# Top 32 of each score row by pair maxima: where the pair minima are made, and which slots search so

## Chip, cores and metric

One core of one Trainium2 chip runs the whole kernel. The metric is device time in microseconds of one execution; lower is better. In the profile the engines are PE (TensorE matmul), PEld (TensorE weight load), DVE (VectorE), ACT (ScalarE), POOL (GpSimd) and SP (the queue that issues most DMAs).

## The reference

Attention in which each query keeps its 32 largest scores, and behind it a two-layer network with a quick GELU. All data are float32.

```python
# q, k, v: (8 batches, 8 heads, 576 positions, 64)
scores = (1 / sqrt(64)) * q @ k.T                      # per batch and head: 576 x 576
kth = np.partition(scores, -32, axis=-1)[..., -32:-31]  # the 32nd largest of each row
scores = np.where(scores >= kth, scores, -1e9)
attn = exp(scores - rowmax);  attn = attn / (rowsum + 1e-9)
x = (attn @ v), heads side by side                     # (4608, 512)
h = x @ w_in                                           # w_in: (512, 2048)
out = (h / (1 + exp(-1.702 * h))) @ w_out              # w_out: (2048, 512)
```

## The kernel before

**Slots.** The attention is cut into 144 slots, 18 for each batch. A slot is 128 query rows of a pair of heads, so it has two score tiles of 128 x 576 (index `i` is 0 or 1). For each slot the kernel makes, in this order:

- `scores(n)` (L297): matmuls into PSUM; `copy_scores(n)` (L309): ScalarE copies them, scaled, into `sc[n]`, two halves `i` of 576.
- The search for the 32 largest scores of each row, on VectorE. MAX8 gives the eight largest of a row, MATCH_REPLACE8 (after a MATCH_VALUE_LOAD) overwrites those eight with a lowest value, so that the next MAX8 finds the next eight.
- `bounds(n)`: two tiny operations on GpSimd that make `cut` (minus the 32nd largest) and `low` (32nd minus largest). `mask(n)` (L426, ScalarE, needs `cut`) and `exps(n)` (L434, ScalarE, needs `low`) make the exponentials `pr` and their row sums `den`.
- `invert(n)` (L442, L444): two tiny VectorE operations turn `den` into `rden`.
- Then normalizing and turning the rows. Up to slot 10 this is `divide` (L451, GpSimd, a diagonal matrix) and matmuls with it; from slot 11 it is `normalize` (L457, GpSimd), `split` (L493, ScalarE), a DMA of `rows` to DRAM and a transposing DMA back into `pt` (L501).
- `values` or `values_at` (L560): matmuls with v.

When four head pairs of a row block are done, the network runs on it in pieces: `hidden` (L621, matmuls with `w_in`), `tanh` (L643, ScalarE, and L646, a copy `h` out of PSUM), `gate` (L655 and L656 on GpSimd, or L658 on VectorE up to slot 10), `project` (L676, matmuls with `w_out`).

**Two kinds of search.** The plain one, `topk`, searches rows of 576: four MAX8 for each half, with three removals between them, the first from `sc` into a tile `left`. It serves slots 0 and 3 to 10. The search by pairs serves slots 1, 2 and 11 to 143 (`by_pairs`). Column k of the first 288 and column k of the last 288 of a row are a pair. `pair_up` makes the pairs' maxima (`greater`) on VectorE (L338), and the minima (`lesser`) on GpSimd in integer arithmetic: a subtract (L342) and, by `pair_rest`, an add (L352). `topk_of_pairs` finds the 32 largest of the maxima (four MAX8 of 288 for each half, three removals) and the 16 largest of the minima (two MAX8, one removal), and joins both lists with two TENSOR_REDUCE: `merge` (L376) and `bound` (L381). `lows` (L402) replaces `bounds` there.

**Order.** The program order on every engine is the order in which the Python code runs (a manual schedule); engines meet only by semaphores. Slots 0 to 10 are issued by `slot(n)`, one after another, with the weights of the network loaded and re-scaled beside them: a raw piece comes by DMA into a buffer of the pool `raws`, ScalarE makes size, sign and low parts (L153, L155, L156), VectorE shifts (L154), GpSimd adds and multiplies (L146, L149; `finish_one`). From slot 11 `two_slots(n)` issues two slots at a time, n odd: `find(n)` and `find(n + 1)` are the searches. Inside `find`, `invert(m - 1)` is put between the searches' operations at a fixed place (`i == 18` or `20` of 23), and `pair_up(m + 1)` too, after the last search of the maxima. In the GpSimd queue of `find(m)` and `measure(m)` stand, in this order, the subtract for m + 1, `normalize(m - 1)`, `lows(m)`, the add for m + 1 and the gate. After slot 143 `last_slot` finishes what is left of the network.

Of the kernel before, what the change touches and what calls it, by code (L numbers as in the profile page):

```python
# [9 lines left out]
ALU = mybir.AluOpType  # L10
# [20 lines left out]
def kernel(  # L31
# [51 lines left out]

    TURNS = 4
    SETTLED = 10
    PAIRED = SETTLED + 1
    EARLY = (1, 2)
    by_pairs = lambda n: n in EARLY or PAIRED <= n < N
    assert D == 64 and 2 * TAIL == P and C == NP * P and C == PIECE and B % 2 == 0
    assert TOPK == 32 and NP == 4 and NF == 4 and NG == 4 and CC == 4  # L90

    const = ctx.enter_context(tc.tile_pool(name="const", bufs=1))
    pool = lambda name, bufs, **kw: ctx.enter_context(tc.tile_pool(name=name, bufs=bufs, **kw))
    raws = pool("raws", 7)
    loads = pool("loads", 2)
    vals = pool("vals", 4)
    qkt = pool("qkt", 6)
    scp = pool("scp", 4)
    prp = pool("prp", 2)
    lefts = pool("lefts", 2)  # L100
    small = pool("small", 4)
    ptp = pool("ptp", 2)
    xs = const.tile([P, 5, CC, P], F32, name="xT")
# [200 lines left out]
    def copy_scores(n):  # L304
        ps = st[n].pop("ps")
        sc = st[n]["sc"] = scp.tile([P, 2, S], F32, name="sc")
        for i in range(2):
            to = sc[:, i, :].rearrange("p (c k) -> p c k", c=2)
            nc.scalar.mul(out=to, in_=ps[i][:, :, 0:HALF], mul=SCALE)  # L309

    def topk(n):

        sc = st[n]["sc"]
        top = st[n]["top"] = small.tile([P, 2, TOPK], F32, name="top")
        left = [lefts.tile([P, S], F32, name="left") for _ in range(2)]
        of = lambda r, i: left[i][:] if r else sc[:, i, :]

        def largest(r, i):
            nc.vector.max(top[:, i, 8 * r : 8 * r + 8], of(r, i))  # L319

        def remove(r, i):
            nc.vector.match_replace(left[i][:], top[:, i, 8 * r : 8 * r + 8], of(r, i), LOWEST)  # L322

        ops = []
        for r in range(TOPK // 8):
            ops += [lambda r=r, i=i: largest(r, i) for i in range(2)]
            if r < TOPK // 8 - 1:
                ops += [lambda r=r, i=i: remove(r, i) for i in range(2)]
        return ops

    greater, lesser = {}, {}

    def pair_up(n):

        sc = st[n]["sc"]
        a, b = sc[:, :, 0:HALF], sc[:, :, HALF:S]
        greater[n] = lefts.tile([P, 2, HALF], F32, name="greater", tag="left")
        nc.vector.tensor_tensor(out=greater[n][:], in0=a, in1=b, op=ALU.max)  # L338
        home, tag = (scp, "sc") if n in EARLY else (raws, "raw")
        lesser[n] = home.tile([P, 2, HALF], F32, name="lesser", tag=tag)  # L340
        whole = lesser[n][:].bitcast(I32)
        nc.gpsimd.tensor_tensor(out=whole, in0=a.bitcast(I32), in1=greater[n][:].bitcast(I32), op=ALU.subtract)  # L342
        unpaired.append(n)

    unpaired = []

    def pair_rest():

        while unpaired:
            n = unpaired.pop()  # L350
            whole, b = lesser[n][:].bitcast(I32), st[n]["sc"][:, :, HALF:S]
            nc.gpsimd.tensor_tensor(out=whole, in0=whole, in1=b.bitcast(I32), op=ALU.add)  # L352

    def topk_of_pairs(n):

        top = st[n]["top"] = small.tile([P, 2, 2 * TOPK], F32, name="top2", tag="top")
        cut = st[n]["cut"] = small.tile([P, 2], F32, name="cut")
        first, few = greater.pop(n), lesser.pop(n)
        left = lefts.tile([P, 2, HALF], F32, name="left2", tag="left")

        def found(r, i, written=False):
            if r < TOPK // 8:
                at = (8 * r + TOPK) % (TOPK + TOPK // 2)
                return top[:, i, at : at + 8]
            end = 2 * TOPK - 8 * (r - TOPK // 8) - TOPK
            return top[:, i, end - 1 : end - 9 : -1] if written else top[:, i, end - 8 : end]

        def largest(src, r, i):
            nc.vector.max(found(r, i, True), src[:, i, :])  # L369

        def remove(to, src, r, i):
            nc.vector.match_replace(to[:, i, :], found(r, i), src[:, i, :], LOWEST)  # L372

        def merge():
            both = top[:, :, 0:TOPK].rearrange("p i (s k) -> p i k s", s=2)
            nc.vector.tensor_reduce(  # L376
                out=top[:, :, TOPK + TOPK // 2 :], in_=both, axis=mybir.AxisListType.X, op=ALU.max
            )

        def bound():  # L380
            nc.vector.tensor_reduce(  # L381
                out=cut[:], in_=top[:, :, TOPK + TOPK // 2 - 1 :], axis=mybir.AxisListType.X, op=ALU.min, negate=True
            )

        ops = []
        for r in range(TOPK // 8):
            ops += [lambda r=r, i=i: largest(left if r else first, r, i) for i in range(2)]
            if r < TOPK // 8 - 1:
                ops += [lambda r=r, i=i: remove(left, left if r else first, r, i) for i in range(2)]
        ops += [lambda: pair_up(n + 1) if PAIRED < n + 1 < N else None]  # L390
        for r in range(TOPK // 8, TOPK * 3 // 16):
            ops += [lambda r=r, i=i: largest(few, r, i) for i in range(2)]
            if r == TOPK // 8:
                ops += [lambda r=r, i=i: remove(few, few, r, i) for i in range(2)]
        return ops + [merge, bound]

    def lows(n):

        top, cut = st[n]["top"], st[n]["cut"]
        low = st[n]["low"] = small.tile([P, 2], F32, name="low")  # L400
        for i in range(2):
            nc.gpsimd.tensor_scalar(  # L402
                low[:, i : i + 1], cut[:, i : i + 1], top[:, i, TOPK : TOPK + 1], -1.0, op0=ALU.add, op1=ALU.mult
            )

    def bounds(n):

        if by_pairs(n):
            return lows(n)
        top = st[n]["top"]  # L410
        cut = st[n]["cut"] = small.tile([P, 2], F32, name="cut")
        low = st[n]["low"] = small.tile([P, 2], F32, name="low")
        nc.gpsimd.tensor_scalar(cut[:], top[:, :, TOPK - 1], -1.0, None, op0=ALU.mult)  # L413
        nc.gpsimd.tensor_tensor(out=low[:], in0=top[:, :, TOPK - 1], in1=top[:, :, 0], op=ALU.subtract)
# [364 lines left out]
    def opening():  # L779

        stay_warm(8, v_ends[0][:].rearrange("p j d -> p (j d)"))
        load("q", 0, 0, nc.sync)
        load("k", 0, 0, nc.scalar)
        for hp in range(2):
            for name in "qk":
                if hp:
                    load(name, 0, hp)
        for x in by_slot[0]:
            load_piece(x)
        prepare_first()  # L790
        scores(0)
        copy_scores(0)
        stay_warm(2)
        for name in "qk":
            prepare(name, 0, 1)
        early.extend(round_piece(x) for x in by_slot[0])
        for piece in early:
            piece["size"]()
        scores(1)
        copy_scores(1)  # L800
        prepare_rest()
        for hp in range(2, NP):
            for name in "qk":
                load(name, 0, hp)
        load_v(0, 0)
        for x in by_slot[1]:
            load_piece(x)
# [11 lines left out]
    def slot(n):  # L819
# [7 lines left out]
        if n == 0:  # L827
            for piece in some:
                piece["low"]()
                piece["sign"]()  # L830
        else:
            if not by_pairs(n):
                bounds(n - 1)
            exponentials(n - 1, bring_all if n % 4 == 1 and n > TURNS + 1 else lambda: None)
            if n == TURNS + 1:
                bring_all()
            copy_scores(n + 1)
            bring_all()
            while signs:
                signs.pop(0)()  # L840
            if 1 < n <= TURNS:
                turn_main(n - 2)
                turn_ends(n - 2)
            for piece in some:
                piece["size"]()
            tanh(False)
        for i, op in enumerate(topk_of_pairs(n) if n in EARLY else topk(n)):
            op()
            if i == 2:
                for _ in range(min(3 if n >= TURNS else 6, len(unfinished))):  # L850
                    finish_one()
            if i == (10 if n in EARLY else 5):
                if n > 0:
                    divide(n - 1)
                while unfinished:
                    finish_one()
            if i == (13 if n == TURNS + 1 else 10):
                gate(False)
        if by_pairs(n + 1):
            bounds(n)  # L860
            pair_up(n + 1)
            pair_rest()
        for piece in some:
            piece["shift"]()
            unfinished.extend(piece["finish"])
# [47 lines left out]
    def two_slots(n):  # L913
# [17 lines left out]
                    fn(*args)  # L931

        def find(m):
            for i, op in enumerate(topk_of_pairs(m) if live(m) else [lambda: None] * 23):
                op()
                if i == (18 if m % 2 else 20) and live(m - 1):
                    invert(m - 1)
                if i > 1 and len(unfinished) > (2 if m == SETTLED + 1 else 0):
                    finish_one()

        def measure(m):
            if live(m):
                lows(m)
            if opens and m == n:
                finish_one()
                finish_one()
                pair_rest()
                return
            pair_rest()
            gate(aside)  # L950
            if m == SETTLED + 4:
                gate(aside)
# [124 lines left out]
```

## Time and profile before

| what | value |
|---|---|
| median of 3 runs | 1452.72 us (1452.57 to 1454.01) |
| profiled execution, first to last instruction (span) | 1451.2 us |
| median of the runs less that span | 1.5 us; no other time is given for the profiled execution |
| granted TensorE clock, mean | 0.991 |
| instructions | 29107 |
| HBM read, written | 45.09 MB, 103.42 MB |

| VectorE or GpSimd group | count | mean ns of one |
|---|---|---|
| MAX8 of 288 columns (L369) | 1620 | 444 to 446 |
| MAX8 of 576 columns (L319) | 72 | 747 to 748 |
| MATCH_REPLACE8 of 288 columns (L372) | 1080 | 439 to 442 |
| MATCH_REPLACE8 of 576 columns (L322) | 54 | 743 |
| TENSOR_TENSOR maximum, 576 columns (L338) | 135 | 986 |
| TENSOR_REDUCE merge, bound (L376, L381) | 135 each | 211, 189 |
| GpSimd subtract, add (L342, L352) | 135 each | 1412 |
| GpSimd normalize (L457) | 268 | 745 |
| GpSimd gate (L655, L656) | 131 each | 617, 1279 |

The mean of one is from its start to its end. The next instruction of the engine can start before that end, so the step from start to start is shorter; the prediction reads it from the timeline. The span begins with some 130 us of slots 0 to 10, goes on with slots 11 to 143 until about 1375 us, and ends with a tail in which TensorE works alone.

### The profile page before, as it was taken

The page shows a single profiled execution, that of the slowest core. Times are in us where ns is not written, and L with a number is a line of the kernel's source. Part 1 is how long each engine was busy: PE and PEld are TensorE (multiplying, and loading weights), DVE is VectorE, ACT ScalarE, POOL GpSimd, SP SyncE. Part 2 cuts the span into 40 slices and gives each one's busy share as a digit, 9 for nine tenths or more (in the row PEclk, how much of TensorE's full clock was granted, in tenths as well). Part 3 has the DMA queues.
Part 4 walks back from the last instruction along what each step waited for, and adds up shares of the span by engine and source line. Part 5 has one row for each costly group of instructions (what it writes and reads, how often), then busy time and mean ns, then how long its engine had stood idle before and what let it go on. Part 6 is the DMA issues. An engine that isn't in the chain of part 4 may idle for free.

```text
span 1451.2 us, 29107 instructions
## 1 busy us (share of the span) xinstructions
PE 1414.1 (97%) x9524; PEld 995.2 (69%) x9524; DVE 1361.8 (94%) x4703; ACT 1159.9 (80%) x1862; POOL 985.2 (68%) x1181
## 2 busy tenths in 40 slices
PE   7889899999999999999999999999999999999998
PEld 5667567777666667777666667777666667777665
DVE  7999999999999999999999999999999999999910
ACT  6998887888888887888888888888878888777730
POOL 4888766676766777766667677766777777667610
PEclk8999999999999999999999999999999999999999
DMA  7542467766777768778677767867677776544430
GB/s 212 162 160 63 139 164 195 184 180 171 190 199 186 176 172 209 188 177 189 167 190 185 186 176 185 209 177 186 163 199 192 183 177 179 163 134 129 137 90 15
DMA packets 521272, 244.40 MB, mean 168 GB/s; under 512 B 457376, under 2 KB 495264, under 8 KB 521120
## 3 DMA queue, kind: packets, MB, share of 16 engines
q1 hardware_dynamic: 520688, 242.25, 64.2%
q8 instruction: 75, 1.23, 0.3%
q14 instruction: 77, 0.63, 0.1%
q10 hardware_dynamic: 432, 0.30, 0.1%
HBM read 45.09 MB, written 103.42 MB: 102 GB/s over the span
## 4 chain that ended last, share of the span: by engine, by line
PE 85%; DVE 11%; ACT 1%; DMA 1%; SPq 1%; issue 1%; POOL 0%; DVEq 0%; POOLq 0%
PE ph L621 33%; PE po L676 31%; PE o L560 10%; PE s_ps L297 10%; DVE top L319 3%; DVE left L322 3%; DVE top L369 2%; DVE left L372 1%; DMA pt<-rows 1%; DVE greater L338 0%; ACT sc L493 0%; DVE lesser L372 0%; DVE wout L154 0%; POOL pr L457 0%; DVE win L154 0%
## 5 line engine op out<-in xcount | busy, mean ns | idle before, releaser
L621 PEld LDWEIGHTS ph<-xT,win 128*128 128x128 f32 x3520 | 484.3, 191 | 86.0 <-issue 54.5
L621 PE MATMUL ph<-xT,win 128*128 128x128 f32 (+1 forms) x3520 | 537.4, 309 | 1.0 <-ACT xT L542 0.6
L676 PE MATMUL po<-wout,th 128*128 128x512 f32 x1152 | 519.3, 593 | 4.9 <-POOL wout L149 3.9
L493 ACT COPY sc<-pr 128x2304 uint16<-128x2304 uint16 x134 | 283.1, 2113 | 163.6 <-POOL pr L457 163.6
L676 PEld LDWEIGHTS po<-wout,th 128*128 128x128 f32 x1152 | 213.0, 190 | 217.8 <-issue 205.1
L369 DVE MAX8 top<-left 128x8 f32<-128x288 f32 x810 | 328.0, 446 | 0.0
L342 POOL TENSOR_TENSOR lesser<-sc,greater 128x576 int32<-128x576 int32 x135 | 190.6, 1412 | 177.1 <-DVE greater L338 177.1
L457 POOL TENSOR_SCALAR pr<-pr,rden 128x576 f32<-128x576 f32 x268 | 196.4, 745 | 127.4 <-DVE top L376 76.8
L372 DVE MATCH_REPLACE8 left<-top,left 128x288 f32<-128x288 f32 x540 | 234.8, 442 | 0.0
L434 ACT ACTIVATE pr<-sc,low 128x576 f32<-128x576 f32 x288 | 220.8, 773 | 0.0
L369 DVE MAX8 top<-lesser 128x8 f32<-128x288 f32 x540 | 218.0, 444 | 0.0
L426 ACT ACTIVATE sc<-sc,cut 128x576 f32<-128x576 f32 x288 | 207.4, 774 | 1.8 <-POOL cut L413 1.7
L309 ACT ACTIVATE sc<-s_ps 128x576 f32<-128x576 f32 x288 | 171.0, 648 | 37.1 <-PE s_ps L297 36.2
L352 POOL TENSOR_TENSOR lesser<-lesser,sc 128x576 int32<-128x576 int32 x135 | 190.6, 1412 | 0.2
L297 PE MATMUL s_ps<-qk_t 64*128 64x288 f32 (+1 forms) x1280 | 182.7, 431 | 0.5 <-ACT qk_t L220 0.5
L656 POOL TENSOR_TENSOR th<-th,h 128x512 f32<-128x512 f32 x131 | 167.6, 1279 | 11.2 <-POOL th L655 0.4
L297 PEld LDWEIGHTS s_ps<-qk_t 64*128 64x128 f32 (+1 forms) x1280 | 99.3, 177 | 78.1 <-issue 60.1
L560 PE MATMUL o<-pt,v_l 128*64 128x128 f32 (+1 forms) x2400 | 145.9, 265 | 3.7 <-DMA pt<-rows 3.5
L560 PEld LDWEIGHTS o<-pt,v_l 128*64 128x64 f32 x2400 | 121.4, 137 | 31.3 <-issue 16.9
L338 DVE TENSOR_TENSOR greater<-sc 128x576 f32<-128x576 f32 x135 | 133.2, 986 | 0.0
L655 POOL TENSOR_SCALAR th<-th 128x512 f32<-128x512 f32 x131 | 80.9, 617 | 58.8 <-ACT th L643 58.8
L643 ACT ACTIVATE th<-ph 128x512 f32<-128x512 f32 x144 | 85.5, 594 | 40.1 <-PE ph L621 35.5
(78 smaller groups left out, 1355.5 us busy)
## 6 DMA issues: line engine op xcount, KB each, us to landing
rows<-sc SPq DMA_DIRECT2D x134, 576.0 KB, 3.2
qk_rows<-halves SPq DMA_DIRECT2D x48, 256.0 KB, 2.8
qk_l<-in_q_dram SPq DMA_DIRECT2D x64, 128.0 KB, 3.4
raw<-in_moe_w_in_dram SPq DMA_DIRECT2D x16, 512.0 KB, 4.6
v_l<-in_v_dram SPq DMA_DIRECT2D x32, 256.0 KB, 3.7
raw<-in_moe_w_out_dram SPq DMA_DIRECT2D x16, 512.0 KB, 3.5
out_dram<-ob SPq DMA_DIRECT2D x32, 256.0 KB, 2.9
qk_l<-in_k_dram SPq DMA_DIRECT2D x62, 128.0 KB, 3.4
```

What stands on the lines that cost most here:

```text
L297: nc.tensor.matmul(ps[i][rows, c, 0:HALF], lhsT=qT[b, hps[p]][on, cols], rhs=kT[b, hps[p]][on, FIRST[i] + c * HALF : FIRST[i] + (c + 1) * ...
L342: nc.gpsimd.tensor_tensor(out=whole, in0=a.bitcast(I32), in1=greater[n][:].bitcast(I32), op=ALU.subtract)
L352: nc.gpsimd.tensor_tensor(out=whole, in0=whole, in1=b.bitcast(I32), op=ALU.add)
L369: nc.vector.max(found(r, i, True), src[:, i, :])
L372: nc.vector.match_replace(to[:, i, :], found(r, i), src[:, i, :], LOWEST)
L426: nc.scalar.activation(sc[:, i, :], sc[:, i, :], AF.Prelu, bias=cut[:, i : i + 1], alpha=HUGE)
L434: nc.scalar.activation(pr[:, i * S : (i + 1) * S], sc[:, i, :], AF.Exp, bias=low[:, i : i + 1], accum_out=den[:, i : i + 1],)
L457: nc.gpsimd.tensor_scalar(pr[:, i, :], pr[:, i, :], st[n]["rden"][:, i : i + 1], 1.0, op0=ALU.mult, op1=ALU.mult)
L493: nc.scalar.copy(out=halves, in_=pr[:].bitcast(U16).rearrange("p (k h) -> p h k", h=2))
L560: nc.tensor.matmul(o[j * D : (j + 1) * D, cols], lhsT=main[:, j, c, :] if c < NF else tail[:, j, :], rhs=pt[:, MAIN[j] + c if c < NF else ...
L621: nc.tensor.matmul(ph[:, i * many * P : (i + 1) * many * P], lhsT=win[:, c, f * P : (f + 1) * P], rhs=xs[:, first : first + step * (many - ...
L676: nc.tensor.matmul(x.po[:], lhsT=gT[:, i * P : (i + 1) * P], rhs=wout[:, f, :], start=(x.done == 0), stop=(x.done == FC - 1))
```

## The change

Every slot now searches by pairs, in one way. `pair_up(n)` writes maxima and minima side by side into one tile `ranked` (per row and half i: 288 maxima, then 288 minima), both by VectorE. `topk(n)` finds the 16 largest of the maxima, removing them in place (both rounds), and then the 16 largest of all 576 that are left, the remaining maxima and the minima. The list of 32 comes out in order, so that the two joins fall away and `bounds` serves every slot. `lesser`, its two GpSimd operations, `merge`, `bound` and `lows` are gone. A pair's minimum can only be among the 32 if its maximum is, so at least 16 of the 32 are maxima, and the result is the same.

The search has 14 operations instead of 23. In `find`, `pair_up(m + 1)` now stands after the eighth of them, and `invert(m - 1)` after the eleventh or the twelfth. In `slot(n)` `pair_up(n + 1)` stands behind the search in every slot, ahead of the shifts of the weights; `divide(n - 1)` stays after the sixth operation, and `bounds(n)` is issued by the next slot, except for slot 10. Before slot 0 a `pair_up(0)` is added. The pool `raws` has 6 buffers instead of 7, and the pool `lefts` gives way to `rank`, two tiles.

```diff
-    PAIRED = SETTLED + 1
-    EARLY = (1, 2)
-    by_pairs = lambda n: n in EARLY or PAIRED <= n < N
-    raws = pool("raws", 7)
+    raws = pool("raws", 6)
-    lefts = pool("lefts", 2)
+    rank = pool("rank", 2)
...
+    ranked = {}
+
+    def pair_up(n):
+
+        sc = st[n]["sc"]
+        a, b = sc[:, :, 0:HALF], sc[:, :, HALF:S]
+        ranked[n] = rank.tile([P, 2, 2, HALF], F32, name="ranked")
+        for c, op in enumerate((ALU.max, ALU.min)):
+            nc.vector.tensor_tensor(out=ranked[n][:, :, c, :], in0=a, in1=b, op=op)
+
     def topk(n):
 
-        sc = st[n]["sc"]
         top = st[n]["top"] = small.tile([P, 2, TOPK], F32, name="top")
-        left = [lefts.tile([P, S], F32, name="left") for _ in range(2)]
-        of = lambda r, i: left[i][:] if r else sc[:, i, :]
+        both = ranked.pop(n)
+
+        def of(r, i):
+            return both[:, i, 0, :] if r < TOPK // 16 else both[:, i, :, :].rearrange("p c k -> p (c k)")
...
-            nc.vector.match_replace(left[i][:], top[:, i, 8 * r : 8 * r + 8], of(r, i), LOWEST)
+            nc.vector.match_replace(of(r, i), top[:, i, 8 * r : 8 * r + 8], of(r, i), LOWEST)
...
-        lesser[n] = home.tile([P, 2, HALF], F32, name="lesser", tag=tag)
-        whole = lesser[n][:].bitcast(I32)
-        nc.gpsimd.tensor_tensor(out=whole, in0=a.bitcast(I32), in1=greater[n][:].bitcast(I32), op=ALU.subtract)
...
-            nc.gpsimd.tensor_tensor(out=whole, in0=whole, in1=b.bitcast(I32), op=ALU.add)
...
-    def topk_of_pairs(n):
...
-    def lows(n):
...
         copy_scores(0)
+        pair_up(0)
...
-            if not by_pairs(n):
-                bounds(n - 1)
+            bounds(n - 1)
...
-        for i, op in enumerate(topk_of_pairs(n) if n in EARLY else topk(n)):
+        for i, op in enumerate(topk(n)):
...
-            if i == (10 if n in EARLY else 5):
+            if i == 5:
...
-        if by_pairs(n + 1):
+        if n == SETTLED:
             bounds(n)
-            pair_up(n + 1)
-            pair_rest()
+        pair_up(n + 1)
...
-            for i, op in enumerate(topk_of_pairs(m) if live(m) else [lambda: None] * 23):
+            for i, op in enumerate(topk(m) if live(m) else [lambda: None] * 14):
                 op()
-                if i == (18 if m % 2 else 20) and live(m - 1):
+                if i == 7 and live(m) and live(m + 1):
+                    pair_up(m + 1)
+                if i == (10 if m % 2 else 11) and live(m - 1):
                     invert(m - 1)
...
-                lows(m)
+                bounds(m)
```

More of the change, by code (lines that the diff above doesn't have):

```diff
@@ L329, in topk @@
         return ops
[L331 to L339, printed above, removed]
-        lesser[n] = home.tile([P, 2, HALF], F32, name="lesser", tag=tag)
-        whole = lesser[n][:].bitcast(I32)
-        nc.gpsimd.tensor_tensor(out=whole, in0=a.bitcast(I32), in1=greater[n][:].bitcast(I32), op=ALU.subtract)
-        unpaired.append(n)
@@ L345 @@
[L345 to L351, printed above, removed]
-            nc.gpsimd.tensor_tensor(out=whole, in0=whole, in1=b.bitcast(I32), op=ALU.add)
-    def topk_of_pairs(n):
[L356 to L395, printed above, removed]
@@ L397, in lows @@
-    def lows(n):
[L399 to L404, printed above, removed]
     def bounds(n):
-        if by_pairs(n):
-            return lows(n)
         top = st[n]["top"]
@@ L946, in measure @@
                 finish_one()
-                pair_rest()
                 return
-            pair_rest()
             gate(aside)
```

## Prediction

> **What bounds the kernel now.** I read the page's busy times and chain first, then the windows, then who waits for whom, then the timeline of single slots. Busy times and the chain that ended last:
>
> ```profile
> PE 1414.1 (97%) x9524; PEld 995.2 (69%) x9524; DVE 1361.8 (94%) x4703; ACT 1159.9 (80%) x1862; POOL 985.2 (68%) x1181
> PE 85%; DVE 11%; ACT 1%; DMA 1%; SPq 1%; issue 1%; POOL 0%; DVEq 0%; POOLq 0%
> ```
>
> TensorE and VectorE are both nearly full, but the chain is TensorE's for 85%. By stage (busy us of PE, PEld, DVE, ACT, POOL, then granted clock, DMA share, GB/s):
>
> ```profile
> 100.00:150.00 50.00, 45.45 (x341) 32.99 (x339) 49.79 (x128) 44.73 (x88) 43.45 (x44) 1.00 0.27 87
> 150.00:200.00 50.00, 45.09 (x343) 31.92 (x344) 49.02 (x178) 39.86 (x73) 36.86 (x44) 0.97 0.59 150
> 300.00:400.00 100.00, 100.00 (x690) 70.43 (x687) 98.59 (x355) 81.47 (x127) 70.28 (x86) 1.00 0.70 176
> ```
>
> A busy TensorE need not be at its peak, so I looked at starts of matmuls: from 241 us to 1369 us they follow each other at a constant step (0.216 us for 256 columns, 0.429 for 512), with no gap over 0.1 us. Two slots take it 18.6 us. There TensorE alone sets the pace, and a faster VectorE buys nothing. From the start to 241 us TensorE does stand still, some 34 us in all, 11 of them after 118 us, and the chain there runs through VectorE. Two of those stops (waiter <- releaser: total, times, longest):
>
> ```profile
> PE po L676 <- POOL wout L149: 3.9, 2, 3.2
> PE o L560 <- DMA pt<-rows: 3.5, 4, 1.3
> ```
>
> So the change is worth what it does to the first 241 us, plus what it may spoil after them.
>
> **VectorE per slot.** Start-to-start steps count, since instructions overlap: 288 wide first, then 576 wide from a plain slot.
>
> ```profile
> 805.30 0.74 DVE L338 TENSOR_TENSOR greater<-sc 128x576 f32<-128x576 f32 x1
> 805.96 0.81 DVE L369 MAX8 top<-lesser 128x8 f32<-128x288 f32 x2
> 806.69 0.07 DVE L372 MATCH_VALUE_LOAD lesser<-top,lesser 128x8 f32 x1
> 806.75 0.44 DVE L372 MATCH_REPLACE8 lesser<-top,lesser 128x288 f32<-128x288 f32 x1
> 807.11 0.08 DVE L372 MATCH_VALUE_LOAD lesser<-top,lesser 128x8 f32 x1
> ...
> 62.45 1.41 DVE L319 MAX8 top<-sc 128x8 f32<-128x576 f32 x2
> 63.78 0.07 DVE L322 MATCH_VALUE_LOAD left<-top,sc 128x8 f32 x1
> 63.84 0.74 DVE L322 MATCH_REPLACE8 left<-top,sc 128x576 f32<-128x576 f32 x1
> 64.50 0.08 DVE L322 MATCH_VALUE_LOAD left<-top,sc 128x8 f32 x1
> ```
>
> MAX8 costs 0.365 us at 288 (0.73 for two) and 0.665 at 576 (1.33 for two); a removal with its load 0.42 and 0.72; the maximum 0.66. A paired slot before: 12 x 0.365 + 8 x 0.42 + 0.66 + 0.35 (two reduces) + 0.27 (inverse) = 9.02, what the timeline shows from 799.85 to 808.87. After: 4 x 0.365 + 4 x 0.42 + 4 x 0.665 + 2 x 0.72 + 2 x 0.66 + 0.27 = 8.83 (ALU.min is not in the trace; an elementwise pass of the same shape, priced as the maximum). The minima that VectorE takes over cost less than the merge, the bound and the shorter searches that it drops. The plain slots (0, 3 to 10) fall from 9.95 to 8.83.
>
> **The port between VectorE and GpSimd.** Every second maximum is long:
>
> ```profile
> 814.32 1.25 DVE L338 TENSOR_TENSOR greater<-sc 128x576 f32<-128x576 f32 x1
> ...
> 812.98 0.62 POOL L655 TENSOR_SCALAR th<-th 128x512 f32<-128x512 f32 x1 [0.90 <-ACT th L643]
> 813.68 1.27 POOL L656 TENSOR_TENSOR th<-th,h 128x512 f32<-128x512 f32 x1
> ...
> 19.19 0.74 DVE L338 TENSOR_TENSOR greater<-sc 128x576 f32<-128x576 f32 x1
> 19.37 1.31 POOL L413 TENSOR_SCALAR cut<-top 128x2 f32<-128x2 f32 x1 [17.69 <-DVE top L319]
> ```
>
> At 814.32 it runs 0.62 us from the end (814.95) of the gate's multiply; alone it takes 0.74. At 19.37 it is the other way: a GpSimd operation on two columns takes 1.31 us, until VectorE's maximum and the two shifts behind it are over, against 0.27 alone. So whoever starts second waits the other out, and VectorE's back-to-back instructions keep the place. Two slots before take 9.02 + 9.67 = 18.69; the 0.65 over two free ones is this wait.
>
> The Trainium skill ("SBUF — State Buffer", Who interferes with whom) says a VectorE instruction with two SBUF inputs and a GpSimd one that reads SBUF exclude each other for the whole instruction, and speaks so against a second two-input pass on VectorE. An estimate by its rule at the worst, each of the four passes in two slots meeting a multiply of 1.28 us, is 17.7 + 5.1 = 22.8 us; the rows show one meeting in two slots.
>
> After, the passes sit 3.15 us into a slot (behind eight searches) instead of 5.45. GpSimd loses 2 x 1.41 us a slot (the subtract and the add). In the slot after an even one's inverse (call its start t) VectorE reaches the passes at t + 0.27 + 1.33 + 3.15 = t + 4.75; the gate's first operation (L655) came at t + 4.72 (808.26 to 812.98), by normalize, split and tanh, none of which change. So they meet: VectorE waits at most 0.58, giving 17.7 to 18.3 for two slots, still below 18.6. GpSimd's delay is the larger: the gate ends at about t + 8.1 instead of t + 6.7. In the other slot the add is gone ahead of the gate and the multiply ends before the passes begin.
>
> **After 241 us: 0.** In the odd slot the passes now come before their scores: the copy that ended at 822.69 had 1.3 us to spare, and the passes come 2.3 us earlier, so VectorE waits there about 0.4 to 1 us per two slots, which is its slack. The queue behind is only its own searches. Bounds (0.46 instead of 0.50 us) follow on a free GpSimd. Nothing that TensorE waits for moves earlier or later, but the gate.
>
> **Up to 241 us: about -4.** Slot 0 now waits for both halves of its scores (10.04 instead of 9.53), then 1.32 + 7.26: ends at 18.7, not 19.2. But the inverse sits at 2.3 us in a plain slot (before 4.1), and waits for the exponentials; these wait for cut on GpSimd, which waits for two passes and the shifts (row 19.37, now in every slot). Loop of a slot: 3.15 (cut, mask, exponentials) + 0.27 + 4.96 (rest of the searches) + 1.32 + 1.0 (shifts) = 10.7, with the gate 11.3. Slots 1 and 2 lose 1.5 together; slots 3 to 10 took 11.25, 10.92, five of 11.5 and 12.2, and gain 0.2 to 0.9 each; ScalarE, at 11.0 us a slot, allows no more. Slot 11 starts some 0.5 us earlier; GpSimd's 1.29 us multiplies on the weights can eat this or more. Slots 11 and 12 took 11.2 and 10.0 because pairing and the last weights crowded GpSimd, where five of its 1.41 us operations go: -1.5. Slots 13 to 20 took 73.9 us, now 8 x 8.83 to 9.15: -0.8 to -3.1, middle -2. The inverse stands 7.25 instead of 8.4 us into a slot: -1.1 for the transposes that TensorE waits for at 240.94. Sum -5; I take -4, since ScalarE follows only in part. The 7 to 6 raw buffers hold a weight piece back by one multiply (about 2.6 us), under 2 us of spare time: 0, at worst 2. The span 1451.2 becomes 1447.2; the median stood 1.5 above the span, so 1448.7.
>
> **Rivals.** *The gate becomes the bound (slower).* Place: TensorE's second project of two slots,
>
> ```profile
> 816.72 3.60 PE L676 MATMUL po<-wout,th 128*128 128x512 f32 x8
> ```
>
> which needs the gate that ended at 814.95, 1.8 us to spare. After, a loop closes: this project + 5.97 to the copied scores + 0.06 + 4.1 (passes, two searches, two removals) to the inverse, + 8.16 to the gate's end, + 0.06 = 18.35 against 18.6. It decides as soon as the gate slips 0.3 us more: a second meeting at the port, or a late th. Price 0.1 to 0.3 us on each of some 62 two-slot rounds, 6 to 19, less the 4: 1455 to 1464, worst 1468. For: margins of 0.3; against: VectorE's own margin grows from nothing to 0.3 to 0.9. 0.33. *The start gives nothing:* cut behind the passes in slots 0 to 10, and multiplies in VectorE's way, take back what slots 11 to 20 gain: 1451 to 1454. For: ScalarE 48 of 50 us busy from 50 to 100 us. 0.2. *The steady stage gets faster with VectorE:* one would expect 1 us per two slots, -60; the unbroken matmuls exclude it; 0.01.
>
> **Numbers.** 0.2% (2.9 us) is about what a measurement of this kernel can tell from no change. Forecast (1445 to 1449.8) 0.46, with the last rival 0.47 faster; 0.2 within; 0.33 slower. The likeliest case's own range is 1445 to 1450; to hold 8 in 10 it must reach into the slower one, 1444.5 to 1464.
>
> **What would show it.** Right: DVE busy falls to about 90% with waits of its TENSOR_TENSOR for ACT's copy; POOL about 600 us (985 less 381 of subtracts and adds); PE still without gaps after 240 us, its stop of 3.2 us for wout gone. Wrong: "po <- POOL th" among TensorE's waits all through the middle (the gate), DVE without a pause at over 9.3 us a slot (the port), or cut above 2 us with TensorE waiting for the turned rows before 120 us (the start).

## The result and the profile after

| kernel | median of the runs | profiled span | ratio to before, 95% interval |
|---|---|---|---|
| before | 1452.72 us (1452.57 to 1454.01) | 1451.2 us | |
| after | 1461.85 us (1461.43 to 1461.98) | 1460.1 us | 1.006 [1.0047, 1.0072] |

The changed kernel is 9.1 us slower. 1448.7 was forecast, 4 us faster; the time lies inside the range of 1444.5 to 1464, on the other side of no change. Busy times and chain of the page after, then its windows (busy us of PE, PEld, DVE, ACT, POOL, granted clock, DMA share, GB/s):

```profile
PE 1419.0 (97%) x9524; PEld 997.2 (68%) x9524; DVE 1311.8 (90%) x3506; ACT 1160.3 (79%) x1862; POOL 684.2 (47%) x911
PE 87%; DVE 8%; ACT 2%; DMA 1%; issue 1%; POOL 1%; POOLq 0%; ACTq 0%; SPq 0%
```

```profile
100.00:150.00 50.00, 47.78 (x386) 36.46 (x382) 47.31 (x114) 43.56 (x88) 41.86 (x38) 1.00 0.36 108
150.00:200.00 50.00, 41.90 (x303) 27.76 (x302) 47.84 (x128) 38.24 (x66) 22.54 (x34) 0.93 0.51 137
300.00:400.00 100.00, 100.00 (x718) 69.44 (x718) 93.63 (x256) 82.78 (x126) 46.75 (x66) 1.00 0.74 182
```

VectorE has 50 us less to do and GpSimd 300, and nothing came of it. The whole loss lies at the start. The table gives when VectorE takes up the search of a slot in the two traces (first MAX8), in us:

| slot | before | after | difference |
|---|---|---|---|
| 0 | 9.53 | 10.80 | +1.27 |
| 3 | 40.28 | 42.92 | +2.64 |
| 10 | 120.11 | 126.97 | +6.86 |
| 13 | 153.51 | 161.20 | +7.69 |
| 21 | 227.40 | 236.44 | +9.04 |
| 40 | 406.15 | 414.64 | +8.50 |
| 57 | 564.64 | 573.54 | +8.90 |

TensorE tells the same: two `project` matmuls stand at 235.8 and 1297.9 us before, and the same two at 244.7 and 1306.7 after, a distance of 1062.1 and 1062.0. From slot 21 on the change is worth nothing, as forecast. What to explain is +9 where the sum had -4. The granted clock is no rival: its mean is lower after (0.984 against 0.991), with the difference in the first 250 us, but a profiled execution below has 0.985 and takes 1452 us.

Who waits for whom after, in slots 0 to 10 (waiter <- releaser: total, times, longest):

```profile
DVE some L373 <- ACT pr L365: 7.4, 9, 1.0
ACT sc L357 <- POOL cut L344: 6.9, 8, 1.1
```

VectorE now waits for the row sums, and ScalarE for `cut`. One slot of that stage in the timeline, with GpSimd's weight operations (L143, L146) between:

```profile
112.42 1.41 DVE L316 TENSOR_TENSOR ranked<-sc 128x576 f32<-128x576 f32 x2
112.61 2.31 POOL L344 TENSOR_SCALAR cut<-top 128x2 f32<-128x2 f32 x1 [0.84 <-DVE top L327]
113.75 1.09 DVE L151 TENSOR_SCALAR wout<-wout 128x512 uint32<-128x512 uint32 x3
114.95 1.44 ACT L357 ACTIVATE sc<-sc,cut 128x576 f32<-128x576 f32 x2 [1.10 <-POOL cut L344]
...
117.66 1.29 POOL L143 TENSOR_TENSOR wout<-wout,raw 128x512 int32<-128x512 int32 x1
118.11 0.87 DVE L373 TENSOR_SCALAR some<-den 128x2 f32<-128x2 f32 x1 [0.96 <-ACT pr L365]
```

`cut`, two columns, takes 2.31 us: until the two passes and the three shifts are over. And `some`, the addition of 1e-9 to two columns of row sums, takes 0.87 us (1.01 to 1.05 in seven of the ten slots), until GpSimd's third weight operation ends at 118.95. The same addition in the kernel before:

```profile
111.49 1.30 POOL L146 TENSOR_TENSOR wout<-wout,raw 128x512 int32<-128x512 int32 x1
112.70 0.15 DVE L442 TENSOR_SCALAR some<-den 128x2 f32<-128x2 f32 x1
```

VectorE came to it later in the slot there, when the third operation was just ending. In slot 4 of the changed kernel, the longest (13.47 us), the two passes (2.17 us instead of 1.41) and the three shifts (2.20 instead of 1.09) are slow as well. Such a stretch, in which an instruction of one of these two engines waits out one of the other, is called a meeting below.

The second place is slots 11 and 12. The two passes take 3.41 us there instead of 1.41, and the projection waits for weights:

```profile
142.08 1.30 POOL L143 TENSOR_TENSOR wout<-wout,raw 128x512 int32<-128x512 int32 x1
142.35 3.41 DVE L316 TENSOR_TENSOR ranked<-sc 128x576 f32<-128x576 f32 x2
143.46 1.69 POOL L146 TENSOR_TENSOR wout<-wout,raw 128x512 f32<-128x512 f32 x1
...
153.35 1.13 PE L607 MATMUL po<-wout,th 128*128 128x512 f32 x2 [1.29 <-POOL wout L146]
153.52 3.40 DVE L316 TENSOR_TENSOR ranked<-sc 128x576 f32<-128x576 f32 x2
...
156.36 1.12 PE L607 MATMUL po<-wout,th 128*128 128x512 f32 x2 [1.88 <-POOL wout L146]
```

The first pass waits out GpSimd's running operation; then GpSimd's next one (143.46) gets in between the two passes, and the second pass waits again.

### The profile page after: what moved, and what is told of

It is laid out like the page before. It is cut to its first block, busy times and chain, and to the rows that moved or that the text cites. A ratio compares the mean times of both kernels' runs of the same rounds, so it can differ in the third digit from the quotient of the medians.

```text
span 1460.1 us, 27372 instructions
## 1 busy us (share of the span) xinstructions
PE 1419.0 (97%) x9524; PEld 997.2 (68%) x9524; DVE 1311.8 (90%) x3506; ACT 1160.3 (79%) x1862; POOL 684.2 (47%) x911
## 4 chain that ended last, share of the span: by engine, by line
PE 87%; DVE 8%; ACT 2%; DMA 1%; issue 1%; POOL 1%; POOLq 0%; ACTq 0%; SPq 0%
PE ph L552 33%; PE po L607 32%; PE o L491 10%; PE s_ps L294 10%; DVE top L327 3%; DVE ranked L330 2%; DVE ranked L316 1%; ACT pr L365 1%; DMA pt<-rows 1%; DVE some L373 1%; ACT sc L357 1%; PE tp L402 0%; POOL cut L344 0%; PE none L168 0%; ACT sc L424 0%
## 5 line engine op out<-in xcount | busy, mean ns | idle before, releaser
L327 DVE MAX8 top<-ranked 128x8 f32<-128x288 f32 (+1 forms) x1152 | 627.7, 596 | 0.0
L330 DVE MATCH_REPLACE8 ranked<-top,ranked 128x288 f32<-128x288 f32 (+1 forms) x864 | 463.4, 543 | 0.0
L316 DVE TENSOR_TENSOR ranked<-sc 128x576 f32<-128x576 f32 x288 | 209.4, 769 | 48.6 <-ACT sc L306 48.5
L586 POOL TENSOR_SCALAR th<-th 128x512 f32<-128x512 f32 x131 | 159.6, 1218 | 153.7 <-ACT th L574 153.7
L344 POOL TENSOR_SCALAR cut<-top 128x2 f32<-128x2 f32 x144 | 49.9, 346 | 60.5 <-DVE top L327 60.5
L577 ACT COPY h<-ph 128x512 f32<-128x512 f32 x131 | 75.9, 579 | 0.0
L330 DVE MATCH_VALUE_LOAD ranked<-top,ranked 128x8 f32 x864 | 65.9, 76 | 0.0
```

The costliest lines, as they stand in the source:

```text
L316: nc.vector.tensor_tensor(out=ranked[n][:, :, c, :], in0=a, in1=b, op=op)
L330: nc.vector.match_replace(of(r, i), top[:, i, 8 * r : 8 * r + 8], of(r, i), LOWEST)
```

## The experiments

Each ratio below is to the kernel before, run again beside it (medians 1452.78 to 1453.08 us).

**First theory, T:** the inverse sets the pace of slots 0 to 10 (a wait of 0.8 us and 0.85 us at the port). **Its rival, U:** the price is `cut`, held behind the passes. Four runs:

*The inverse later.*

```diff
-            if i == 5:
+            if i == 9:
                 if n > 0:
                     divide(n - 1)
```

> One edit to the changed kernel: in the slots up to 20, VectorE takes up the inverse of the sums (and the remaining weight operations) behind the tenth operation of the search instead of behind the sixth. Theory T (the inverse sets the pace of slots 0 to 10: VectorE waits 0.80 us there for the row sums and then needs 1.02 us instead of 0.15 for two columns, because GpSimd's third weight operation runs at that moment): both go, 1.6 us of VectorE's loop in each of about ten slots, until ScalarE's own loop (about 11.0 to 11.3 us a slot) is what remains; 5 to 7 us faster than the changed kernel, about 1455 to 1457, and the addition to the sums costs 0.15 to 0.2 us in nearly all of these slots. Theory U (the price is the cut, held behind the two passes and the shifts for 1.98 to 2.32 us instead of about 0.7, and ScalarE late by that): the passes and the cut stand where they were, so within 1.5 us of 1461.9; the copies that take the transposes away come later by the delay, which could even cost 1 to 3 us.

Measured: 1462.05 us, 1.0068 [1.0054, 1.0082]: nothing gained, though wait and slow addition are gone:

```profile
119.94 0.14 DVE L373 TENSOR_SCALAR some<-den 128x2 f32<-128x2 f32 x1
123.58 2.52 DVE L316 TENSOR_TENSOR ranked<-sc 128x576 f32<-128x576 f32 x2
123.77 1.71 POOL L146 TENSOR_TENSOR wout<-wout,raw 128x512 f32<-128x512 f32 x1
125.45 0.72 POOL L344 TENSOR_SCALAR cut<-top 128x2 f32<-128x2 f32 x1
126.02 2.19 DVE L151 TENSOR_SCALAR wout<-wout 128x512 uint32<-128x512 uint32 x3
```

The put-off weight operations run later too, and now the passes (2.52 instead of 1.41 us) and the shifts (2.19 instead of 1.09) wait for GpSimd. T fell as it was put. U's number held, but not its mechanism: `cut` starts later, takes 0.72 us and so ends 2.6 us after the passes began, as late as before (2.5), yet VectorE no longer waits for the sums that depend on it, and the slot got longer, 12.67 instead of 12.21. Slot 11 starts 1.6 us later than in the changed kernel and takes 9.75 us instead of 11.18, which gives most of that back.

*Two weight operations instead of three ahead of the inverse.*

```diff
-                for _ in range(min(3 if n >= TURNS else 6, len(unfinished))):
+                for _ in range(min(2, len(unfinished))):
```

> One edit to the changed kernel: behind the third operation of the search only two of the put-off weight operations are given to GpSimd instead of three (six in the first slots), the rest together with the inverse. The third operation then no longer runs when VectorE adds to the sums; the wait of 0.80 us for the sums stays. Theory T: the addition falls from 1.02 to 0.15 us, 0.85 us in each of about ten slots, less what the later weight operations may cost where they meet the passes (up to 0.45 us a slot): 3 to 6 us faster, about 1456 to 1459. Theory U: no change to the cut behind the passes, so within 1 us of 1461.9.

Measured: 1461.71 us, 1.0057 [1.0045, 1.007]. The same: U's number held, T's did not. The addition takes 0.15 us, and the time comes back at the passes (1.98 us) and the shifts (2.18):

```profile
119.88 0.15 DVE L373 TENSOR_SCALAR some<-den 128x2 f32<-128x2 f32 x1
...
125.68 1.98 DVE L316 TENSOR_TENSOR ranked<-sc 128x576 f32<-128x576 f32 x2
127.59 2.18 DVE L151 TENSOR_SCALAR wout<-wout 128x512 uint32<-128x512 uint32 x3
```

*The passes inside the search*, so that `cut` is not behind them.

```diff
+            if i == 7:
+                pair_up(n + 1)
...
-        pair_up(n + 1)
```

> One edit to the changed kernel: in the slots up to 20 the two passes for the next slot are made behind the eighth operation of the present search instead of behind its end, so that GpSimd's cut no longer stands behind them. Theory U: ScalarE gets the cut about 1.3 us earlier in each of ten slots, 8 to 13 us faster, about 1449 to 1454. Theory T: VectorE has the same work in its loop and still waits for the sums, now with the passes to fill part of the wait in some slots, but they can meet GpSimd's weight operations (0.5 to 1.0 us): between 3 us faster and 3 us slower than 1461.9.

Measured: 1470.15 us, 1.0118 [1.0104, 1.0131], 8.3 us slower than the changed kernel. U had forecast 8 to 13 us faster, T within 3: both fell.

```profile
111.06 1.02 DVE L373 TENSOR_SCALAR some<-den 128x2 f32<-128x2 f32 x1 [0.79 <-ACT pr L365]
113.03 2.52 DVE L316 TENSOR_TENSOR ranked<-sc 128x576 f32<-128x576 f32 x2
113.13 1.80 POOL L146 TENSOR_TENSOR wout<-wout,raw 128x512 f32<-128x512 f32 x1
...
120.34 0.98 POOL L344 TENSOR_SCALAR cut<-top 128x2 f32<-128x2 f32 x1 [2.24 <-DVE top L327]
```

`cut` is down to 0.98 us, as in the kernel before, while the wait, the slow addition and a meeting of the passes now add up. The shorter `cut` brings VectorE nothing: it ends 0.15 us after the next search begins (121.32, the search at 121.17), as in the changed kernel (114.92 and 114.76), because the passes left the place between the two searches as well. The same run again:

> The changed kernel with the two passes behind the eighth operation of the search, once more, as a second sample beside the runs of this batch: both theories expect 1469 to 1471 and 13.3 us a slot.

Measured: 1469.88 us, 13.3 us a slot, the same.

*The plain search in slots 0 to 10.*

```diff
     def pair_up(n):
+        if n <= SETTLED:
+            return
...
+            if plain:
+                return whole(i) if r else st[n]["sc"][:, i, :]
```

> One edit to the changed kernel: slots 0 to 10 search all 576 columns of a row in four steps, with no passes, as slots 0 and 3 to 10 of the kernel before do; from slot 11 on the changed search stays. This parts the loss by its place. From the two traces the first pass or search of slot 10 starts 6.9 us later than before and that of slot 21 9.0 later, so slots 0 to 10 hold 6.9 and slots 11 to 20 2.1. With slots 3 to 10 as before (4.2 us back) and slots 1 and 2 without any pairing (they lose 1.5 us each against before) 1455 to 1459 is expected. If the whole loss lay behind slot 11 (the passes of slots 11 and 12 that meet GpSimd twice), it would stay at 1460 to 1462 or go up by the 3 us of slots 1 and 2; if it lay wholly in slots 3 to 10, 1454 to 1456.

Measured: 1456.59 us, 1.0026 [1.0016, 1.0036]. Slot 10 starts 1.3 us later than before instead of 6.9, slot 21 4.1 instead of 9.0. So 5 to 6 us of the loss belong to slots 0 to 10 and about 3 to slots 10 to 20.

**Second theory, T2.** The four runs fit one account. VectorE's own instructions in one of these slots, start to start, are 10.45 us in every form: searches 2.31 + 0.85 + 1.33 + 0.72 + 0.73 + 1.33, inverse 0.26, gate 0.59, passes 1.32, shifts 1.01. The rest of a slot is what VectorE loses:

| kernel (slot read) | wait for row sums | at the inverse | at the passes | at the shifts | own + lost | slot |
|---|---|---|---|---|---|---|
| after (9) | 1.04 | 0.72 | 0 | 0 | 12.21 | 12.21 |
| inverse later (9) | 0 | 0 | 1.12 | 1.10 | 12.67 | 12.67 |
| two weight operations (9) | 0 | 0 | 0.59 | 1.09 | 12.13 | 12.12 |
| passes inside (8) | 0.88 | 0.87 | 1.12 | 0 | 13.32 | 13.29 |

GpSimd is busy for 42 of the 50 us from 100 to 150, so there is hardly a moment at which a pass, a shift or a two-column operation does not find it at work. Moving one of them only moved the meeting in these runs. Rival V: the new search is too long in itself. To part them, GpSimd's weight operations were taken out of both kernels:

```diff
-            nc.gpsimd.tensor_tensor(out=whole, in0=whole, in1=low.bitcast(I32), op=ALU.add)
...
-            nc.gpsimd.tensor_tensor(out=dst, in0=dst, in1=high, op=ALU.mult)
```

> The kernel before with GpSimd's two weight operations of each piece (the addition and the multiplication of the weights' rounding) left out, so the weights come out unfinished; all else stays. It is the base for the next run. VectorE's search reads no tensor pair there, and its small operations cost 0.15 to 0.17 us already: 11.2 to 11.5 us a slot in slots 3 to 10, as before. The stalls of the projection for finished weights at 147 and 152 us (0.9 and 3.5 us) go: 1446 to 1452.

Measured: 1453.92 us, 1.0006 [0.9996, 1.0015]. Slots about as expected (slot 10 starts at 120.93), the total 1.9 us above the range: the stalls for weights gave way to others (3.0 us for the copied scores, 2.3 for the output's copy).

> The changed kernel with the same weight operations of GpSimd left out. Theory T2, formed after the first four runs (VectorE's own instructions take about 10.4 us a slot now, against 11.2 to 11.5 before, but 0.85 to 2.2 us a slot are added wherever one of its passes, shifts or two-column operations meets GpSimd at work; moving an operation only moves the meeting): the addition to the sums falls to 0.15 us, slots 3 to 10 take 11.0 to 11.4 us instead of 12.2 (the round through the cut and ScalarE, 2.5 + 3.1 + 0.3 + 5.5 = 11.4 us, is next), the stalls for weights behind slot 11 go; 1447 to 1453, within 3 us of the kernel before treated alike. Theory V (the new search is too long in itself, or the held cut alone sets the pace): slots 3 to 10 stay at about 12.2 us and it stays 6 to 9 us behind the kernel before treated alike.

Measured: 1454.12 us, 1.0008 [0.9998, 1.0017]. The total lies 1.1 us above the range of T2, but the two kernels are equal without GpSimd's weight operations (0.2 us apart); the 9 us are gone, and V, as a search too long in itself, with them. Slot 10 starts at 120.06 us (before, treated alike, at 120.93); slots 7 to 9 take 11.0 to 11.2 us (slots 3 to 10 10.7 to 12.7):

```profile
106.50 1.41 DVE L316 TENSOR_TENSOR ranked<-sc 128x576 f32<-128x576 f32 x2
107.09 0.22 POOL L344 TENSOR_SCALAR cut<-top 128x2 f32<-128x2 f32 x1 [5.38 <-ACT raw L153]
107.83 1.09 DVE L151 TENSOR_SCALAR wout<-wout 128x512 uint32<-128x512 uint32 x3
111.56 0.17 DVE L373 TENSOR_SCALAR some<-den 128x2 f32<-128x2 f32 x1 [0.34 <-ACT pr L365]
```

This pair of runs alone doesn't part the meetings from the held `cut` and from TensorE's waits for weights, since all of them go at once. The runs with the passes inside the search part the `cut`, and the last ones below leave GpSimd's work in place.

*The passes of slots 11 and 12 later.*

```diff
-                if i == 7 and live(m) and live(m + 1):
+                if i == (11 if m <= SETTLED + 2 else 7) and live(m) and live(m + 1):
```

> One edit to the changed kernel: in slots 11 and 12 the two passes for the next slot come behind the twelfth operation of the search instead of behind the eighth, so that GpSimd has finished its weight operations when they run. In the changed kernel these two pairs of passes take 3.4 us each instead of 1.41, and the projection waits 1.35 and 1.94 us for weights and 3.2 us behind them. If these meetings cost the 2 us that the kernel loses behind slot 10: 2 to 4 us faster than 1461.9, 1458 to 1460. If the projection's waits come from the lateness of slot 10 alone: within 0.7 us of 1461.9.

Measured: 1458.43 us, 1.0039 [1.0025, 1.0054]: 3.4 us less than the changed kernel's median, as expected, though the intervals of the two ratios overlap. The passes are back to 1.56 and 1.41 us. From slot 11 to slot 14 the trace, of the slowest of the five executions (1460.61 us), gains 2.9 us, of which 1.4 are left at slot 21.

**What makes a pass wait.** The gate on VectorE (one operand in PSUM, one in SBUF) takes 0.68 us beside GpSimd all the time. So the passes were given one operand from PSUM, where the scores come from. This run and the rest have plain transfers in place of the DMA transposes of the later stage; the changed kernel and the kernel before were run in that form as well.

> The changed kernel with the DMA transposes of the stage behind slot 11 left out: two plain transfers of the high halves of the numbers take the place of each, so what TensorE then multiplies is not the turned rows. It is the base for the next runs of this form. Slots 0 to 10 issue none of them, so their starts should stay within 1 us of the changed kernel's (slot 10 at 126.97 us); behind them TensorE sets the pace, and the total should stay within 5 us of 1461.9.

Measured: 1459.25 us; slot 10 at 126.93 us.

> The kernel before in the form with plain transfers, for the comparison of whole times within this form: slot 10 at 120 us as in the kernel before, and 7 to 10 us faster than the changed kernel in this form.

Measured: 1451.59 us, 0.9992 [0.9982, 1.0001]; slot 10 at 120.98. The gap in this form is 7.7 us.

*Passes inside the search, one operand from PSUM.*

```diff
+            for i in range(2):
+                nc.vector.scalar_tensor_tensor(
+                    out=ranked[n][:, i, c, :], in0=st[n]["kept"][i][:, 0, 0:HALF], scalar=SCALE,
+                    in1=sc[:, i, HALF:S], op0=ALU.mult, op1=op,
+                )
```

> The form with plain transfers, and the passes within the search (behind its eighth operation) as in the run that took 13.3 us a slot and 1470 us, but in the slots up to 10 a pass takes one operand from the scores in PSUM, scaled on the way, as the gate takes its hidden units, and only the other from SBUF (four operations of 288 columns instead of two of 576). All of GpSimd's work in these slots stays. Theory T2a (a pass waits for GpSimd because both its operands lie in SBUF; the gate, with one operand in PSUM, takes 0.68 us beside GpSimd's operations): the passes fall from 2.52 to about 1.5 us, 12.3 us a slot; the wait of 0.8 us and the slow addition of 1.02 us stay. Theory T2b (any operation of VectorE that starts beside GpSimd's weight operations waits): the passes stay above 2.3 us and the slot at 13.3.

Measured: 1461.16 us, 12.3 us a slot. T2a's numbers hold, T2b's do not:

```profile
107.50 1.01 DVE L380 TENSOR_SCALAR some<-den 128x2 f32<-128x2 f32 x1 [0.79 <-ACT pr L372]
109.47 1.54 DVE L320 SCALAR_TENSOR_TENSOR ranked<-s_ps,sc 128x288 f32<-128x288 f32 x4
109.57 1.29 POOL L146 TENSOR_TENSOR wout<-wout,raw 128x512 f32<-128x512 f32 x1
```

A GpSimd operation runs through the passes; they take 1.54 us, where the same place cost 2.52 with both operands in SBUF, and GpSimd's operation takes 1.29, where it took 1.80. This agrees with the Trainium skill ("SBUF — State Buffer", Who interferes with whom): a VectorE instruction with two SBUF inputs contends with a GpSimd instruction that reads SBUF, one with a single SBUF input outside the two-port modes does not. Two limits: the run changed the instruction and its size along with the operand's place, and the new instruction was not run with both operands in SBUF; and the addition and the shifts, which met GpSimd too, have a single tensor operand each, so the count of SBUF operands alone does not tell which instructions meet.

*All of it together:* the inverse and the PSUM passes behind the tenth operation, and the later passes in slots 11 and 12.

> The form with plain transfers, and all that the runs point to at once: in the slots up to 10 the inverse and the passes for the next slot come behind the tenth operation of the search, the passes with one operand from PSUM; in slots 11 and 12 the passes come behind the twelfth operation. All of GpSimd's work stays. Theory T2 (VectorE's own 10.4 us a slot and what it meets): wait, slow addition and meetings are gone, about 10.6 us a slot for VectorE, and ScalarE's 11.0 to 11.3 us is next; slot 10 starts at about 117 to 121 us instead of 127, and slot 21 another 2 to 3 us earlier; in all 9 to 13 us faster than the changed kernel in this form. If the transposes on TensorE, which start 2.3 us later in a slot, or ScalarE set the pace at 12 us or more: 2 to 5 us faster, all of it behind slot 10.

Measured: 1451.82 us, 0.9994 [0.9985, 1.0004], 7.4 us faster than the changed kernel in this form (9 to 13 were expected) and level with the kernel before in it (1451.59). Slot 10 starts at 120.45 us, as expected; slots 7 to 9 take 11.0 to 11.3 us. ScalarE is busy for 48.5 of the 50 us from 50 to 100, so it is probably next; no run tests that. All of GpSimd's work is in place:

```profile
113.73 0.15 DVE L380 TENSOR_SCALAR some<-den 128x2 f32<-128x2 f32 x1
114.00 1.58 DVE L320 SCALAR_TENSOR_TENSOR ranked<-s_ps,sc 128x288 f32<-128x288 f32 x4
114.93 1.30 POOL L146 TENSOR_TENSOR wout<-wout,raw 128x512 f32<-128x512 f32 x1
```

It does not beat the kernel before: repaired, the change gains nothing. Three edits are in this run at once, so it shows that they are enough together, not what each gives.

**Are the two losses separate?** The plain start with the later passes of slots 11 and 12:

> The form with plain transfers; slots 0 to 10 search all 576 columns as in the run with the plain start (which gave 5.3 us), and in slots 11 and 12 the passes come behind the twelfth operation (which alone gave 3.4 us). If the two losses are separate: 8 to 9 us faster than the changed kernel in this form, 1450 to 1452. If the second gain came only because slot 11 started late: 5 to 6 us faster, 1453 to 1455.

Measured: 1452.19 us, 0.9993 [0.9984, 1.0002]: 7.1 us gained, between the two cases. The losses are mostly separate; part of the second gain is given back before slot 21, as above.

**Is VectorE spare behind 241 us?**

```diff
+            if n > SETTLED + 14 and c == 0 and n % 2:
+                nc.vector.tensor_tensor(out=ranked[n][:, :, c, :], in0=a, in1=b, op=op)
```

> The form with plain transfers of the changed kernel (1459.25 us), with one more pass of 0.665 us (a repetition of the maxima) in every second slot from slot 25 on, 60 passes and 40 us of VectorE in all. If TensorE alone sets the pace there (18.6 us for two slots, VectorE 17.7): within 1.5 us of 1459.25. If VectorE is the bound there, or its end lets the next slot begin: 1485 to 1499.

Measured: 1478.38 us, 1.0174 [1.0157, 1.0191]: 19.1 us more than 1459.25, so neither case. Of 0.665 us more in two slots, 0.32 (19.1 over 60 rounds) reach the time; the round grows from 18.75 to 19.10 us (slots 30 to 130). TensorE's waits between 300 and 1300 us show one that the changed kernel in this form does not have there:

```profile
PEld po L610 <- POOL th L590: 16.9, 33, 0.6
PE po L610 <- POOL th L590: 4.1, 23, 0.2
```

This is the loop of the prediction's gate rival: 18.35 us, with the pass 19.02. VectorE's spare time is about 0.35 us a round (0.665 less 0.32), not the 0.9 that a sum of its own instructions gives. That the loop closes through the gate is read from these waits; no run gave GpSimd a faster gate.

## Why the prediction went wrong

Point by point:

- **The stage behind 241 us: right.** Forecast 0, and TensorE's matmuls keep their distance (1062.1, 1062.0 us). VectorE's share is 90%, and a slot of it takes 8.84 us where no wait stands (forecast 8.83). It waits 48.5 us in all for ScalarE's copies, as said.
- **The gate rival: did not happen, but is real.** The gate's first operation does meet the passes (its mean goes from 617 to 1218 ns), VectorE is not delayed, and TensorE waits for a gate only once, 0.2 us. With 0.665 us more the loop closes, so the margin was sized about right: 0.25 forecast, some 0.35 measured, in rounds of 18.75 us on average (the one that the prediction read took 18.6). GpSimd's 684 us instead of some 604 (985 less 381) fit these meetings: 131 x 0.6 = 79.
- **Slots 0 to 10: the step that failed.** The loop was 3.15 + 0.27 + 4.96 + 1.32 + 1.0, with the gate 11.3 us. It is 12.2 in slots 7 to 10. Slots 3 to 10 were to gain 0.2 to 0.9 us each and lost 4.3 in all (96.3 us, before 92.0); slots 1 and 2 lost 3.1, not 1.5. The term mis-sized in the loop is the inverse: 0.27, measured 0.98 in slot 9 (118.11 to 119.09) and up to 1.16. Cut, mask and exponentials took 3.35 for 3.15; the other terms held. But a right figure there alone would not have saved the forecast, since two runs took that cost away for nothing. The fault is one step earlier: the port was priced for the passes in the stage of two slots, where GpSimd has 47 of 100 us to do, and for `cut`; at the start, with GpSimd at 42 of 50, the sum gave VectorE's operations free passage (that the multiplies "can eat this or more" stands beside it without a term). The runs showed meetings of 0.6 to 1.1 us each in its place, one or two of them in a slot. Row 19.37, which the prediction read, shows the other side of it: there GpSimd waited for VectorE.
- **"VectorE's back-to-back instructions keep the place": not always.** In row 112.61 `cut` waits for two passes and three shifts. Without GpSimd's weight operations it ends 0.81 us after the passes begin, in the run with all edits together in 0.30 us beside three shifts; and where the first pass had to wait, GpSimd's next operation goes in between. The last is what turned -1.5 for slots 11 and 12 into a loss: slot 11 to slot 13 took 22.01 us, before 21.23, with TensorE stalled 1.29, 1.88 and then 3.17 us for an output's copy. The stop of 3.2 us for weights, which was to go, only changed its shape.
- **Slots 13 to 20, -2, and the inverse there, -1.1: not seen.** Slot 13 to slot 21 took 75.24 us, before 73.89. VectorE's slots are 8.84, but it then waits for copied scores (1.99 us at 192.94, 1.35 at 213.04). TensorE, late by then, is what the copies wait for; a stage in which VectorE was no bound was given a gain of VectorE's.
- **The start rival** named the place, a cut held above 2 us and TensorE waiting for the turned rows, and "multiplies in VectorE's way", but as a loss of the gain only (1451 to 1454, 0.2). The held cut is not what costs: with `cut` at 0.98 us and the passes inside the search the slots were longer, not shorter. A case in which the meetings cost more than the whole saving was missing.
- **The raw buffers, 0 and at worst 2: no cost seen.** Two runs with 6 buffers come level with the kernel before (1451.82 and 1452.19 us against 1451.59 in the same form).
- **The range held by luck.** 1461.85 lies inside 1444.5 to 1464 because the range was stretched for the gate rival, which did not happen.

## What to carry to other kernels

Before an elementwise step with two SBUF operands moves to VectorE, look at how busy GpSimd is at that very place: at 84%, as here, every such instruction has to be priced with a meeting (0.6 to 1.1 us), and so have the shifts and the two-column addition, which have one tensor operand. If GpSimd cannot be emptied, try the step with an operand from PSUM (1.54 us instead of 2.52 here), and check with a run that takes the other engine's work away rather than by moving the step about, since a moved step finds the next meeting.

## What the runs showed of the hardware

- An addition on two columns took 1.01 to 1.05 us on VectorE instead of 0.15 when it started beside a GpSimd operation of 1.29 us. Three shifts took 2.18 to 2.20 us instead of 1.09. The small size of the addition did not protect it.
- Between two passes of VectorE that stand directly behind each other GpSimd's next operation got in where the first pass had waited (two passes 3.41 us, GpSimd's 1.69). Where it hadn't, `cut` stayed behind five VectorE instructions in most slots of the changed kernel (2.31 us). The Trainium skill ("SBUF — State Buffer", Who interferes with whom) gives the shared ports to whoever issues first, for one instruction; the rows agree with that for single instructions. Why `cut` waited for five of them, but in the run without weight operations was done 0.81 us after the passes began, no run here settles.
- MAX8 and MATCH_REPLACE8 showed no meeting in the traces before and after: 0.365 and 0.42 us a step (the removal with its load) at 288 columns, 0.665 and 0.72 at 576, beside GpSimd's work too.
